# Forming each difference product at its own token in a kernel of two attention layers

## The chip, the core and the metric

The kernel runs on one core of a Trainium2 chip. A core has a matrix engine (PE), a vector engine (DVE), a scalar engine (ACT), a general engine (POOL) and a queue engine (SP) that issues transfers. Each works through its own instructions in order, and they wait for one another by semaphores. The metric is the device time of one execution in microseconds (us).

## The reference

Two attention layers read the same input, 2048 tokens of width 576, in 32 heads of width 18. Layer A is ordinary multi-head attention; layer B has queries per head and one shared key and value. A gate per token mixes the two.

```python
def _A_ref(x, wqkv, wo):
    B, S, D = x.shape
    H = 32; Dh = D // H
    qkv = ...                                   # (3, B, H, S, Dh)
    q, k, v = qkv[0], qkv[1], qkv[2]
    scores = jnp.einsum("bhqd,bhkd->bhqk", q, k) * Dh ** -0.5
    p = _softmax(scores, axis=-1)
    o = jnp.einsum("bhqk,bhkd->bhqd", p, v)
    return o.transpose(0, 2, 1, 3).reshape(B, S, D) @ wo
# _B_ref: the same with k = x @ wk and v = x @ wv shared by all heads
g = _sigmoid((x * gate_w).sum(-1, keepdims=True))
return g * a + (1 - g) * b
```

## The kernel before, in words

A head of either layer is a unit `u`, 64 in all: 0 to 31 of layer B, 32 to 63 of layer A. A unit has 16 steps, so there are 1024 steps.

Softmax needs a maximum per query row, and it is found by its own pass over the scores. For step M (128 queries of a unit) four products of 54 x 128 by 54 x 512 give the scores against all 2048 keys, 512 keys each. The DVE reduces each product to one maximum per query (`tensor_reduce` into `mx`, L634). The DVE has less room than it would need for this, so every even step hands part of it to ACT. The keys of quarter 1 minus those of quarter 0 lie ready (`kd`); the product with them, the **difference product**, is the score difference. ACT takes its relu into `xb` (L628; two buffers), and the DVE then reads the plain product of quarter 0, adds `xb` and takes the maximum in one instruction (L631): max(a, b) = a + relu(b − a). A pair of steps thus needs one difference product (`x`), one product of quarter 0 that is added to it (`y`), and six plain ones (`m`).

The second pass, LEAD = 22 steps behind, forms the scores again, transposed, four products of 56 x 512 per step (`s`, L670; two extra rows subtract the maximum), lets ACT take the exponential into `pt` (L678), and multiplies `pt` with the values into the accumulator bank `acc` (L685). That last product, here called the sums, is cut into quarters of 128 columns.

PE works in two modes. For scores and maxima the array is split in two halves by rows: the `s` products lie in the lower half, `x`, `y` and `m` in the upper one, and two products run side by side. For the sums it is split into four by columns. Products leave PE through seven banks of the accumulator memory; the eighth is `acc`. Projections of layer A and the output projection are woven in as **units of work**: either as half products on both halves of the array (`A` and `B`, L882, two banks held open), or whole (`U`, 12 products that use all 128 rows, L863).

**What sets the order.** The program is written out in order by hand: `emit` (L1061) reads a string of tokens, one letter per product and a digit for that many quarters of sums. One string covers 8 steps of scores and 4 pairs of maxima, and one pass over it is here called an **emission**; a **group** is the stretch of tokens up to and with a digit. The loop of L1120 runs 125 emissions: 2 PLAIN, 32 HALF14, 1 PLAIN, 42 HALF14, 2 PLAIN, 32 HALF12, 7 PLAIN, 7 DENSE. HALF14 and HALF12 carry one unit of work as half products, DENSE four whole ones, PLAIN none. Groups counted below are those of the strings: group 5 of HALF14 is the long one with most `A` and `B`, group 7 is "yssmsm 2"; group 7 of HALF12 is the long one.

**Where x and y stand in the code.** In `emit`, an `x` token forms a difference product only if none is open (L1072, `pos["x"] == pos["y"]`); if one is open the token does nothing. A `y` token first forms a difference if none is open, and then its own product. `step_max` (L613) writes the product and the instruction that empties its bank.

**Which bank a product takes.** `Clock` (L45) keeps an estimate of when each of the seven banks comes free, from fixed times for a product, an exponential and a reduction; `bank` (L87) takes the one that is free first and books the new use on ACT or the DVE. A `y` is booked as a plain `m`, without its difference. The estimate runs only while the program is written. On the chip a product waits for its bank's last reader, and as PE works in order, everything behind it waits too.

Other work that hangs on the emissions: at fixed steps `begin` issues loads of queries, keys and differences (SP), pieces of normalising (DVE, POOL, SP) and the weights of the output projection.

Of the kernel before, what the change touches and what calls it, by code (L numbers as in the profile page):

```python
# [38 lines left out]
class Unit:  # L39
    def __init__(self, ops, n, dst, done, view=lambda f: f, how="copy"):  # L40
        self.ops, self.n, self.dst, self.done, self.view, self.how = ops, n, dst, done, view, how
        self.left, self.fp = {"a": 0, "b": 0}, {}


class Clock:  # L45


    def __init__(self):
        self.free = [0.0] * 7
        self.t = self.act = self.dve = self.last = 0.0  # L50
        self.mode, self.begun, self.tail = "", [0.0, 0.0], [0.0, 0.0]
        self.turns, self.count, self.held = {"s": 0, "m": 0}, 0, {}

    def turn(self, which):
        n = self.turns[which]
# [30 lines left out]

    def bank(self, what, tile):  # L87
        k, free = self.first()
        if what in "smx":
            s = self.matmul(tile, free, STREAM)  # L90
            act = what != "m"
            self.leave(k, s, act, EXP_T if act else RED_T, EXP_D if act else RED_D)
        else:
            if self.mode == "s":
                self.t = max(self.tail)
            s = max(self.t, free) + (LOAD + 14 * (HALF_MM + 11) if what != "t" else STREAM)
            self.t, self.mode = s + 99, ""
            self.leave(k, s - STREAM, what == "U", COPY_T, COPY_T + 90)
        return k
# [33 lines left out]
def gated_mix_kernel(ctx: ExitStack, tc: tile.TileContext, xT, wall, wv, wo, out):  # L133
# [45 lines left out]
    clk = Clock()  # L179

    def bank_tile(k):
        return ps_b.tile([P, 512], F32, name=f"bank{k}")

    def in_turn(which):
        return bank_tile(clk.turn(which))
# [118 lines left out]
    def run(gen):  # L304
        for _ in gen:
            pass
# [295 lines left out]
    def kst(u):  # L602
        return ksb if u < H else L["ks"][(u - H) % 3]
# [7 lines left out]
    MX = {}  # L611

    def step_max(u, i, c, low=False, which=None):  # L613

        if u not in MX:
            MX[u] = mxs[u] if u < 2 else mxs[2 + u % 3]
        b = SB if low else MB
        if c == "x":  # L620
            k = L["kd", u if u >= H else 0][b:b + 54, :]
        else:
            k = kst(u)[b:b + 54, c * 512:(c + 1) * 512]
        pm = in_turn(which) if which else bank_tile(clk.bank("x" if c == "x" else "m", 1))
        nc.tensor.matmul(pm, qs[u % 3][b:b + 54, i * P:(i + 1) * P], k, start=True, stop=True)  # L625
        if c == "x":
            MX["x", u, i] = lead.tile([P, 512], F32, name="xb", bufs=2)
            nc.scalar.activation(MX["x", u, i], pm, AF.Relu)  # L628
        elif c == 0 and ("x", u, i) in MX:
            junk = lead.tile([P, 512], BF16, name="junk", bufs=1)  # L630
            nc.vector.tensor_tensor_reduce(junk, pm, MX.pop(("x", u, i)), 1.0, -3e38, op0=OP.add, op1=OP.max,  # L631
                                           accum_out=MX[u][:, i, c:c + 1])
        else:
            nc.vector.tensor_reduce(MX[u][:, i, c:c + 1], pm, axis=AX.X, op=OP.max)  # L634
# [22 lines left out]
    def bank(n):  # L657


        u, r = divmod(n, 64)  # L660
        if u < NU - 1:
            return u, r // 4, r % 4
        half, r = divmod(r, 32)
        return u, r // 2, 2 * half + r % 2

    def step_scores(u, i, c, alone, k):

        b = MB if alone and k % 2 else SB
        ps = in_turn("s") if alone is None else ring("s", b == SB)
        nc.tensor.matmul(ps, kst(u)[b:b + 56, i * P:(i + 1) * P],  # L670
                         qs[u % 3][b:b + 56, c * 512:(c + 1) * 512], start=True, stop=True)
        PT["q"] = PT.get("q", []) + [(c, ps)]
        if alone and k == 0:
            return
        for c, ps in PT.pop("q"):
            n = PT["n"] = PT.get("n", -1) + 1
            pt = L["pt"][n % 14 > 3].tile([P, 512], F32, name="pt")
            nc.scalar.activation(pt, ps, AF.Exp, scale=SCALE)  # L678
            PT[u, i, c] = pt
# [262 lines left out]
    NSTEP = 16 * NU  # L942
# [6 lines left out]
    def next_unit():  # L949
        while todo:  # L950
            u = next(todo[0], None)
            if u is not None:
                return u
            todo.pop(0)
# [36 lines left out]
    def keep_busy():  # L991

        for n in (512, 256):
            nc.tensor.matmul(acc[:, 0:n], ident_r[SB:SB + 56, :], ident_r[SB:SB + 56, 0:1].to_broadcast([56, n]),
                             start=True, stop=True, skip_group_check=True)

    def first_steps(ops):

        for op in ops.replace(" ", ""):
            if op == "f":  # L1000
                keep_busy()
            elif op == "s":
                step_scores(*bank(pos["s"]), None, 0)
                pos["s"] += 1
            else:
                M, c = banks.pop(0)
                step_max(*divmod(M, 16), c, op == "l", "m")
# [3 lines left out]
    pos = {"s": 0, "P": 0, "x": (LEAD + 2) // 2, "y": (LEAD + 2) // 2}  # L1011
    for v in range(16):
        if v == 11:
            max_rows(0)
        mt, c, w = next(left)
# [24 lines left out]
    PLAIN = "mssmsm 4 smsmsm 3 smmssx 3 smmsys 3 mssxysm 3 msxmssm 3 mssysms 3 msssmys 4 msmsms 3 smxssm 3"  # L1040
    HALF14 = "ysmssm 4 xsmsms 4 sysmms 4 sAmsAsAsm 3 msAsmBBAABsAABABmsABABmsABABmBBAxBBBx 1 smsysm 4 yssmsm 2 msms 2 msmsms 4 sxsmms 4"
    HALF12 = "mssmsx 4 mssmsm 4 smssyms 4 msmssm 4 msmssm 4 sysmms 3 mssAAmBAAsAABsAABmBsAABmBBABAxBBmBBysxs 3 smsysm 3 smsmxs 3"
    DENSE = "Umssysm 4 smsmsm 3 smsx 5 msmsmsUsxmssy 5 smsmsmUmssyms 4 smsmms 4 sxmssm 7 smsmmsUsyxsms"
    plain = [(M, c) for p in range((LEAD + 2) // 2, NSTEP // 2)
             for M, c in [(2 * p, 2), (2 * p, 3)] + [(2 * p + 1, c) for c in range(4)]]

# [14 lines left out]
    def emit(ops, units=0):  # L1061
        for op in ops.replace(" ", ""):
            if op == "s":
                if pos["s"] % 8 == 0:
                    begin(pos["s"] // 4)
                step_scores(*bank(pos["s"]), pos["s"] // 4 >= NSTEP - LEAD, pos["s"] % 4)
                pos["s"] += 1
            elif op == "f":
                keep_busy()
            elif op in "xy":  # L1070

                if pos["x"] == pos["y"] and 2 * pos["x"] < NSTEP:  # L1072
                    step_max(*divmod(2 * pos["x"], 16), "x")
                    pos["x"] += 1
                if op == "y":
                    step_max(*divmod(2 * pos["y"], 16), 0)
                    pos["y"] += 1
            elif op == "m":
                M, c = plain.pop(0)
                step_max(*divmod(M, 16), c)  # L1080
            elif op in "AB":
                if units:
                    half_step(op.lower())
            elif op == "U":
                u = next_unit() if units else None
                if u:
                    whole_unit(u)
                    units -= 1
            elif op == "V":
                whole_unit(next(out_last))  # L1090
            elif op in "abc":
                if op == "a":
                    while slow:
                        run(slow.pop(0))
                    L["half"] = last_sums(pos["P"] // (4 * NSTEP))
                next(L["half"])
                if op == "a" and not pos["P"] // (4 * NSTEP):
                    next(out_last)
            else:
                n = 1 if op == "P" else int(op)  # L1100
                while n:
                    last, h = divmod(pos["P"], 4 * NSTEP - 64)
                    if last:
                        k = min(n, 2 - h % 2)
                        last_pv(h // 32, h % 32 // 2, 128 * (h % 2), 128 * (h % 2 + k))
                    else:
                        T, a = divmod(pos["P"], 4)
                        k = min(n, 4 - a)
                        step_pv(*divmod(T, 16), 128 * a, 128 * (a + k))
                    pos["P"] += k  # L1110
                    n -= k
                    if pos["P"] % 64 == 0 and pos["P"] < 4 * NSTEP:
                        head_out(pos["P"] // 64 - 1)
# [3 lines left out]
    open_ph2()  # L1117
    begin(0)
    first_steps("smf smf smf smf")
    while pos["s"] < 4 * (NSTEP - LEAD):  # L1120
        T = pos["s"] // 4
        if (T + LEAD) % 16 == 0 and (T + LEAD) // 16 - 1 < NU:
            max_rows((T + LEAD) // 16 - 1)
        if T >= SEG[1][3] + 4:
            emit(DENSE, 4)
        elif VB <= T < VB + 8 * 32 or RB <= T < RE:
            emit(HALF14, 1)
        elif SEG[0][3] + 4 <= T < SEG[0][3] + 4 + 8 * 32:
            emit(HALF12, 1)
        else:  # L1130
            emit(PLAIN)
# [45 lines left out]
```

## Time and profile before

| | |
|---|---|
| median of three runs | 2784.67 us (2784.38 to 2785.37) |
| the profiled execution | 2785.18 us, its span 2783.4 us |
| granted clock of TensorE | 1.00 |
| before the loop's first scores | about 135 us |
| the 125 emissions | from about 135 to 2714 us |
| the end (last scores, sums, projection) | 69.5 us |

The page gives busy time per engine as a share of the span. A PE that is busy is not PE at its peak: products of the two halves overlap, and a product that waits for its bank shows as a late load of weights (PEld) behind an idle time. The chain of waits is the work that ended last, followed back; it is read in order of time, each row with its start, its length, the engine, what it writes and its line. In the timeline a row has start, length, engine, line, operation, tiles and shapes, the count merged, and in brackets the idle time of the engine before it and what ended it.

### The profile page before, as it was taken

To read this page: it belongs to the slowest core of one execution; us is meant where nothing else is said; L and a number is where in the kernel's file an instruction comes from. 1 tells how busy PE (TensorE), PEld (TensorE's weight loads), DVE (VectorE), ACT (ScalarE), POOL (GpSimd) and SP (SyncE) were. 2 spreads that over 40 slices of the span, in tenths; PEclk is the share of its full clock that TensorE was granted. 3 is DMA by queue.
4 is the path that set the end of the run, shared out by engine and by line. 5 is a ranking of instruction groups with operands and counts; after the bars stand their busy time and mean duration, and the time that the engine had idled before them with its cause. 6 is when DMAs were issued, how large, how long until landed. Compare 5 with 4: busy or idle time off the path is not lost.

```text
span 2783.4 us, 61929 instructions
## 1 busy us (share of the span) xinstructions
PE 2759.3 (99%) x23256; PEld 1367.6 (49%) x23256; DVE 2427.6 (87%) x4559; ACT 2440.9 (88%) x4787; POOL 425.5 (15%) x633
## 2 busy tenths in 40 slices
PE   9999999999999999999999999999999999999999
PEld 7644444444444444444444444454444544445555
DVE  5889999999999999999999999899888988998773
ACT  4399999999999999999999999999999999997776
POOL 2710000010003112322222122000100010101002
PEclk9999999999999999999999999999999999999999
DMA  8821111321124344434555453222321231233312
GB/s 275 331 64 57 56 48 46 82 70 44 57 67 148 110 125 139 134 121 134 167 159 174 132 147 122 83 72 85 101 80 58 81 99 57 70 95 108 99 37 88
DMA packets 190128, 293.71 MB, mean 106 GB/s; under 512 B 54738, under 2 KB 149282, under 8 KB 178252
## 3 DMA queue, kind: packets, MB, share of 16 engines
q1 hardware_dynamic: 170564, 224.02, 27.5%
q0 software_dynamic: 18368, 64.50, 6.2%
q8 instruction: 183, 3.00, 0.4%
q10 hardware_dynamic: 896, 1.23, 0.1%
q14 instruction: 117, 0.96, 0.1%
HBM read 203.29 MB, written 77.62 MB: 101 GB/s over the span
## 4 chain that ended last, share of the span: by engine, by line
PE 88%; DVE 6%; ACT 3%; issue 2%; DMA 1%; POOL 0%; SPq 0%; ACTq 0%; POOLq 0%; DVEq 0%
PE acc L685 34%; PE bank L670 21%; PE bank L625 21%; PE bank L882 7%; DVE junk L631 3%; ACT xb L628 3%; PE bank L863 2%; PE bank L251 2%; DVE mx L634 2%; ACT pt L678 1%; PE acc L697 0%; DMA qs<-qk 0%; SPq L139 0%; DMA qk<-phl 0%; PE bank L361 0%
## 5 line engine op out<-in xcount | busy, mean ns | idle before, releaser
L678 ACT ACTIVATE pt<-bank 128x512 f32<-128x512 f32 x4096 | 2147.8, 609 | 208.1 <-PE bank L670 112.7
L634 DVE TENSOR_REDUCE mx<-bank 128x1 f32<-128x512 f32 x3096 | 1965.2, 684 | 119.1 <-PE bank L670 61.7
L670 PE MATMUL bank<-qs,ksb 56*128 56x512 f32 x2688 | 913.5, 430 | 8.2
L625 PE MATMUL bank<-ksb,qs 54*128 54x512 f32 x2364 | 799.6, 420 | 2.4 <-DVE mx L631 1.0
L670 PEld LDWEIGHTS bank<-qs,ksb 56*128 56x128 f32 x2688 | 438.7, 184 | 279.6 <-DVE mx L634 158.1
L685 PE MATMUL acc<-pt,vb 128*19 128x512 f32 (+3 forms) x5240 | 565.8, 506 | 0.0
L685 PE MATMUL acc<-pt,vg 128*19 128x256 f32 (+3 forms) x5688 | 537.2, 469 | 0.0
L625 PEld LDWEIGHTS bank<-ksb,qs 54*128 54x128 f32 x2364 | 399.1, 184 | 246.4 <-ACT pt L678 130.3
L670 PE MATMUL bank<-qs,ksa 56*128 56x512 f32 x1408 | 468.3, 434 | 3.7 <-DVE ksb L215 0.5
L631 DVE CUSTOM_DVE_ANT_0 junk<-bank,xb 128x512 bf16<-128x512 f32 x500 | 343.2, 686 | 136.8 <-ACT xb L628 94.3
L625 PE MATMUL bank<-ksa,qs 54*128 54x512 f32 x1232 | 425.8, 425 | 1.8 <-DVE mx L631 1.1
L628 ACT ACTIVATE xb<-bank 128x512 f32<-128x512 f32 x500 | 305.8, 612 | 34.4 <-PE bank L670 33.6
L670 PEld LDWEIGHTS bank<-qs,ksa 56*128 56x128 f32 x1408 | 223.7, 184 | 144.4 <-ACT pt L678 56.4
L625 PEld LDWEIGHTS bank<-ksa,qs 54*128 54x128 f32 x1232 | 207.1, 184 | 151.0 <-ACT pt L678 84.0
L213 POOL CAST mh<-mt 128x32 fp32r<-128x32 f32 x64 | 13.5, 211 | 1470.6 <-DVE mt L643 1470.6
L685 PEld LDWEIGHTS acc<-pt,vg 128*19 128x19 f32 x5688 | 110.6, 97 | 202.3 <-issue 180.0
L685 PEld LDWEIGHTS acc<-pt,vb 128*19 128x19 f32 x5240 | 90.3, 97 | 195.0 <-issue 182.1
L625 PE MATMUL bank<-kdb,qs 54*128 54x512 f32 x372 | 170.3, 458 | 0.0
L882 PE MATMUL bank<-xr,wrh 64*128 64x292 f32 (+1 forms) x756 | 145.7, 300 | 0.0
L625 PEld LDWEIGHTS bank<-kdb,qs 54*128 54x128 f32 x372 | 68.5, 184 | 115.9 <-ACT pt L678 56.0
L882 PEld LDWEIGHTS bank<-xr,wrh 64*128 64x128 f32 x756 | 124.6, 186 | 0.1
L882 PE MATMUL bank<-vwh,xv 64*128 64x288 f32 x576 | 109.4, 298 | 0.0
(142 smaller groups left out, 1917.8 us busy)
## 6 DMA issues: line engine op xcount, KB each, us to landing
qs<-qk SPq DMA_DIRECT2D x384, 144.0 KB
xr<-x_d SPq DMA_DIRECT2D x36, 1314.0 KB
ksa<-qk SPq DMA_DIRECT2D x132, 144.0 KB
qk<-phl POOLq DMA_DIRECT2D x32, 512.0 KB, 5.4
qk<-rhl POOLq DMA_DIRECT2D x36, 292.0 KB, 3.3
ksb<-qk SPq DMA_DIRECT2D x66, 144.0 KB
xv<-x_d SPq DMA_DIRECT2D x16, 576.0 KB
onh<-oh POOLq DMA_DIRECT2D x32, 256.0 KB, 3.7
```

The costliest lines, as they stand in the source:

```text
L213: eng_h.tensor_copy(h, src)
L251: nc.tensor.matmul(fp[:, p0:p0 + g], w[a][:kr, k, :], X[b][:kr, k, x0 + p0:x0 + p0 + g], start=(n == 0), stop=(n == len(PROJ) - 1))
L625: nc.tensor.matmul(pm, qs[u % 3][b:b + 54, i * P:(i + 1) * P], k, start=True, stop=True)
L628: nc.scalar.activation(MX["x", u, i], pm, AF.Relu)
L631: nc.vector.tensor_tensor_reduce(junk, pm, MX.pop(("x", u, i)), 1.0, -3e38, op0=OP.add, op1=OP.max, accum_out=MX[u][:, i, c:c + 1])
L634: nc.vector.tensor_reduce(MX[u][:, i, c:c + 1], pm, axis=AX.X, op=OP.max)
L670: nc.tensor.matmul(ps, kst(u)[b:b + 56, i * P:(i + 1) * P], qs[u % 3][b:b + 56, c * 512:(c + 1) * 512], start=True, stop=True)
L678: nc.scalar.activation(pt, ps, AF.Exp, scale=SCALE)
L685: nc.tensor.matmul(acc[32 * j:32 * j + 19, a:b], v_of(u, i), PT[u, i, j][:, a:b], start=(i == 0), stop=(i == 15), skip_group_check=True)
L863: nc.tensor.matmul(fp[:, 0:u.n], x, y, start=(n == 0), stop=(n == len(u.ops) - 1))
L882: nc.tensor.matmul(u.fp[op][:, 0:u.n], x[b:b + 64], y[b:b + 64], start=(n == 0), stop=(n == len(u.ops) - 1))
```

## The change

An `x` token now forms a difference product whether or not one is open, so up to two are ahead, as many as there are `xb` buffers; one is formed ahead of the loop, and only a `y` token still looks whether one is open. The bank estimate has a kind `y` of its own: it keeps a list of the times at which it reckons the relus to be done, and a `y` starts on the DVE no earlier than its own. The strings PLAIN, HALF14 and HALF12 are as before. DENSE is rewritten as four equal pairs.

```diff
     def bank(self, what, tile):
         k, free = self.first()
-        if what in "smx":
+        if what in "smxy":
             s = self.matmul(tile, free, STREAM)
-            act = what != "m"
+            act = what in "sx"
+            if what == "y" and self.diffs:
+                self.dve = max(self.dve, self.diffs.pop(0))
             self.leave(k, s, act, EXP_T if act else RED_T, EXP_D if act else RED_D)
+            if what == "x":
+                self.diffs.append(self.free[k])
...
-        pm = in_turn(which) if which else bank_tile(clk.bank("x" if c == "x" else "m", 1))
+        pm = in_turn(which) if which else bank_tile(clk.bank("x" if c == "x" else "y" if c == 0 and ("x", u, i) in MX else "m", 1))
...
-    DENSE = "Umssysm 4 smsmsm 3 smsx 5 msmsmsUsxmssy 5 smsmsmUmssyms 4 smsmms 4 sxmssm 7 smsmmsUsyxsms"
+    DENSE = "smsysm 4 smsmsmUsmsx 4 smsysm 4 smsmsmUsmsx 4 smsysm 4 smsmsmUsmsx 4 smsysm 4 smsmsmUsmsx 4"
...
-                if pos["x"] == pos["y"] and 2 * pos["x"] < NSTEP:
+                if (op == "x" or pos["x"] == pos["y"]) and 2 * pos["x"] < NSTEP:
                     step_max(*divmod(2 * pos["x"], 16), "x")
                     pos["x"] += 1
...
     first_steps("smf smf smf smf")
+    emit("x")
     while pos["s"] < 4 * (NSTEP - LEAD):
```

The strings that keep their text:

```python
PLAIN = "mssmsm 4 smsmsm 3 smmssx 3 smmsys 3 mssxysm 3 msxmssm 3 mssysms 3 msssmys 4 msmsms 3 smxssm 3"
HALF14 = "ysmssm 4 xsmsms 4 sysmms 4 sAmsAsAsm 3 msAsmBBAABsAABABmsABABmsABABmBBAxBBBx 1 smsysm 4 yssmsm 2 msms 2 msmsms 4 sxsmms 4"
HALF12 = "mssmsx 4 mssmsm 4 smssyms 4 msmssm 4 msmssm 4 sysmms 3 mssAAmBAAsAABsAABmBsAABmBBABAxBBmBBysxs 3 smsysm 3 smsmxs 3"
```

More of the change, by code (lines that the diff above doesn't have):

```diff
@@ L51, in __init__ @@
         self.mode, self.begun, self.tail = "", [0.0, 0.0], [0.0, 0.0]
-        self.turns, self.count, self.held = {"s": 0, "m": 0}, 0, {}
+        self.turns, self.count, self.held, self.diffs = {"s": 0, "m": 0}, 0, {}, []
     def turn(self, which):
```

## The prediction

> **What bounds the kernel now.** I read the page's totals first, then the waits, then the busy time by stage, and last the chain of work inside one emission of each pattern.
>
> ```profile
> PE 2759.3 (99%) x23256; PEld 1367.6 (49%) x23256; DVE 2427.6 (87%) x4559; ACT 2440.9 (88%) x4787; POOL 425.5 (15%) x633
> ...
> PE 88%; DVE 6%; ACT 3%; issue 2%; DMA 1%; POOL 0%; SPq 0%; ACTq 0%; POOLq 0%; DVEq 0%
> PE acc L685 34%; PE bank L670 21%; PE bank L625 21%; PE bank L882 7%; DVE junk L631 3%; ACT xb L628 3%; PE bank L863 2%; PE bank L251 2%; DVE mx L634 2%; ACT pt L678 1%; PE acc L697 0%; DMA qs<-qk 0%; SPq L139 0%; DMA qk<-phl 0%; PE bank L361 0%
> ```
>
> PE is busy 99% and carries 88% of the chain. But the chain leaves PE for one pair of instructions: the relu of a difference (ACT xb L628, 3%) and the DVE maximum that reads it (junk L631, 3%). 3% of 2783.4 us is 83 us, at 0.69 us each some 120 passages: about one in each of the 125 emissions. The waits say the same:
>
> ```profile
> DVE junk L631 <- ACT xb L628: 94.3, 122, 1.2
> ```
>
> 122 of the 500 `y` products wait for their difference, 0.77 us each. The stages show how much room each engine has:
>
> ```profile
> core 0: us, PE busy (x) PEld busy (x) DVE busy (x) ACT busy (x) POOL busy (x), PEclk, DMA share, GB/s
> 176.40:824.80 648.40, 645.12 (x5506) 305.14 (x5504) 590.84 (x1113) 599.55 (x1185) 26.61 (x55) 1.00 0.19 57
> 844.90:1697.10 852.20, 847.97 (x7226) 400.42 (x7224) 776.14 (x1462) 787.06 (x1556) 201.98 (x303) 1.00 0.47 141
> 1737.20:2392.70 655.50, 653.10 (x5634) 315.85 (x5633) 588.54 (x1112) 601.25 (x1185) 48.46 (x81) 1.00 0.27 79
> 2392.70:2513.00 120.30, 118.38 (x1107) 53.55 (x1104) 108.25 (x204) 110.94 (x217) 15.33 (x20) 1.00 0.28 78
> 2534.70:2713.90 179.20, 178.16 (x1446) 98.86 (x1442) 138.99 (x260) 131.33 (x252) 7.69 (x13) 1.00 0.24 74
> ```
>
> These are 32 and 42 emissions of HALF14, 32 of HALF12, 6 of PLAIN and 7 of DENSE: 20.26, 20.29, 20.48, 20.05 and 25.60 us each. Of 20.29 us ACT is busy 787.06/42 = 18.74 and DVE 776.14/42 = 18.48. Both have about 1.5 us to give in an emission, so PE, with what it waits for, sets the length. The granted clock is 1.00 in every stage.
>
> **Where the wait sits in HALF14.** The chain inside one emission, from the first product of group 7 on:
>
> ```profile
> 1202.24 0.42 PE bank L625
> ...
> 1202.70 0.61 ACT xb L628
> ...
> 1203.33 0.69 DVE junk L631
> ...
> 1204.03 0.61 DVE mx L634
> ...
> 1204.69 0.50 PE bank L670
> 1205.19 0.56 PE acc L685 x8
> 1205.75 0.43 PE bank L625
> ...
> 1206.18 0.23 PE bank L625
> ...
> 1206.64 0.98 PE acc L685 x8
> 1207.62 0.43 PE bank L670
> ```
>
> An undisturbed group of six products (three on each half of the array) takes 1206.64 − 1205.75 = 0.89 us, and four quarters of sums 0.98. A step of one product on each half is 0.23, so four products take 0.66; two quarters take 0.56. Groups 7 and 8 ("yssmsm 2", "msms 2"; before, an `x` is formed just ahead of the `y`) should take 0.89 + 0.56 + 0.66 = 2.11 us to the start of the second sums. They take 1205.19 − 1202.24 = 2.95. The loss is 0.84 us: the seventh product on a half that already had three (0.23), and the DVE that stands until the relu is done, so that the next banks come free late.
>
> **The change, part by part.**
>
> *No work is added.* `x` and `y` stay 500 each, as do all maxima, exponentials, whole units and DMAs; the list of open differences exists only while the program is written. The `x` ahead of the loop replaces a later one. No queue gets a new transfer, and the first `x` of a new unit is in both versions the last `x` token of an emission, so the loads of queries and keys are as early against it as before: no price for SP's or POOL's queue. POOL only splits operands and adds halves; nothing of it moves.
>
> *HALF14 (74 emissions).* The tokens run y x y x x y y x, starting with one difference open. Before, the second of the two neighbouring `x` (end of group 5, "BBAxBBBx") did nothing, and the `y` of group 7 made its own. After, that `x` is formed in group 5 and the `y` of group 7 finds it ready. Gain at most 0.84. Given back: one product more at the end of group 5, beside half products on the other half of the array; I take half a step, 0.10. And ACT gets a second relu just there, 0.49 us later than its exps would start (the pitch below), which group 6 with three exps in 1.87 us does not quite absorb; I take 0.20 for a bank that comes late in group 7. That leaves 0.54. DVE is late next: with five maxima in groups 7 and 8 (5 × 0.63 = 3.1 us for 2.67 us of PE), it falls 0.45 behind, which seven banks should cover and group 10 with two maxima makes good.
>
> ```profile
> 1203.95 5.70 DVE L634 TENSOR_REDUCE mx<-bank 128x1 f32<-128x512 f32 x9
> ...
> 1209.12 2.57 ACT L678 ACTIVATE pt<-bank 128x512 f32<-128x512 f32 x5
> ```
>
> (Pitch of ACT (2.57 − 0.61)/4 = 0.49; of DVE (5.70 − 0.68)/8 = 0.63.) Bounds: 0.23 if only the balance of the halves is won, 0.84 if nothing is given back. 74 × 0.54 = 40 us, bounds 17 and 62.
>
> *HALF12 (32).* The tokens run x y y x y x y x. Now the first `x` is formed in group 1 (two ahead), and the `y` of group 6 ("sysmms 3") needs none.
>
> ```profile
> 2073.85 0.43 PE bank L670
> ...
> 2074.87 0.60 ACT xb L628
> ...
> 2075.50 0.69 DVE junk L631
> ...
> 2076.25 0.73 PE bank L670 x2
> 2076.98 0.41 PE bank L882 x3
> ...
> 2080.52 0.78 PE acc L685 x16
> ```
>
> Without the wait group 6 takes 0.89 and its three quarters 0.78 (the sums of group 7 are three quarters too); group 7 starts at 2073.85 + 1.67 = 2075.52, and its first two scores are done at 2075.52 + 0.66 = 2076.18, where the trace has 2076.98: a loss of 0.80. Against it stands ACT: group 7 has seven exps, two relus and a copy, 10 × 0.49 = 4.9 us, on 4.9 us of PE (2080.52 − 0.80 − 2075.52 = 4.2, and 0.78 of sums), and the relu moved into group 1 comes right behind groups 8 and 9 with seven ACT instructions (3.4 us) in 3.4 us. I take off 0.2: 0.6 each, bounds 0.3 and 0.8. 32 × 0.6 = 19 us, bounds 10 and 26.
>
> *PLAIN (12).* Two `y` of four follow their `x` at once now (groups 5 and 8).
>
> ```profile
> 2461.13 0.49 PE L625 MATMUL bank<-ksb,qs 54*128 54x512 f32 x1
> ...
> 2461.28 0.69 DVE L631 CUSTOM_DVE_ANT_0 junk<-bank,xb 128x512 bf16<-128x512 f32 x1 [0.80 <-ACT xb L628]
> ...
> 2463.06 0.84 PE L685 MATMUL acc<-pt,vg 128*19 128x384 f32 x8
> ...
> 2465.75 0.50 PE L625 MATMUL bank<-ksb,qs 54*128 54x512 f32 x1
> ...
> 2467.50 1.06 PE L685 MATMUL acc<-pt,vg 128*19 128x256 f32 x16
> ```
>
> Seven or eight products stand in 1.93 and 1.75 us, where 0.89 + 0.23 = 1.12 do: 0.81 and 0.63, 1.44 together. ACT caps it: 110.94/6 = 18.49 busy of 20.05 leaves 1.56. With both engines nearly full I take 1.1, bounds 0.5 and 1.5: 13 us (6 to 18).
>
> *DENSE (7).* The new order is "smsysm 4" and "smsmsmUsmsx 4", four times. A whole unit, and five quarters of sums:
>
> ```profile
> 2592.12 1.79 PE bank L863 x12
> ...
> 2594.80 1.20 PE acc L685 x16
> ```
>
> A pair costs 0.89 + 0.98, then 0.89 + 1.79 + 0.66 + 0.98, together 6.19; four are 24.76 against 25.60. Gain 0.84, 7 × 0.84 = 6 us. Eight runs of sums stand where seven stood. A quarter costs (0.98 − 0.56)/2 = 0.21 (five, 1.20, agree), so a run costs 0.98 − 4 × 0.21 = 0.14 and 0.20 for the longer first step after it (0.43 against 0.23): 0.34 × 7 = 2.4 us, and the 6 us already contain it. The Trainium skill, TensorEngine Tiling (Array Packing), section Key Properties, says that changing the tiling mode drains TensorE, which speaks against this order; by that rule and these rows the DENSE term is 6, and without it 8. The trace agrees: the first product after sums takes 0.43, the later ones 0.23. Bounds 0 (the banks held over a unit run short) and 8 (no price for the run).
>
> *The bank estimate* now lets a `y` hold its bank until its difference is there, and puts DVE's later work behind that. No instruction, but every later choice of bank can differ. The trace of before has no row for it. Nearest rows: an undisturbed step waits 0; a bank that came late cost 0.42 of idle before the load:
>
> ```profile
> 1204.69 0.18 PEld L670 LDWEIGHTS bank<-qs,ksb 56*128 56x128 f32 x1 [0.42 <-DVE mx L634]
> ```
>
> So between −0.42 and +0.42 us per emission and wrong (or mended) choice. I take 0: in the undisturbed groups the present estimate already lets no bank come late, and the new one differs only where a difference is pending.
>
> **The sum.** 40 + 19 + 13 + 6 = 78 us off the profiled execution's 2785.2: 2707, and 0.5 less against the median of 2784.67: 2706. With every loss recovered 62 + 26 + 18 + 8 = 114: 2671.
>
> **The rivals.**
>
> *R1: the wait moves to ACT.* The relus now come in bursts (two in group 5 of HALF14, one before group 2 of HALF12), where ACT has least room, and PE waits for an exp's bank instead. For it: 18.74 of 20.29 us busy. Then the lower bounds hold, 17 + 10 + 6 and 2 in DENSE, 35 us: 2750. The Trainium skill, TensorEngine Tiling (Array Packing), section PSUM Bottleneck, says that tiling speeds up TensorE but not the emptying of PSUM, which may become the bottleneck; over a whole emission the row leaves 1.55 us above ACT, more than the 0.84 sought, so the rule can bind here only for a few groups.
>
> *R2: slower, by the choice of banks.* PE issues in order, so one product whose bank is still held stops both halves and the sums behind it. Price 0.42 a time; the gain of 78 us over 106 HALF emissions is 0.74 each, so from two such waits in every emission on the change loses. With two it is 2785 + 106 × 0.84 − 78 = 2796, with three 2840; I name 2815. Against it: nothing of the kind stands in the undisturbed groups now.
>
> *R3: hidden.* If PE's 99% were all work, nothing would move: 2785. Against it: 0.77 us on 122 occasions, and loads that take 49%.
>
> **How the numbers follow.** The forecast, 2671 to 2730, has 0.60; R1, 2730 to 2770, has 0.24; R3 0.04; R2 0.12. A change of 0.2% (5.6 us) is about what this kernel's measurement tells from none. Faster is 0.60 + 0.24 = 0.84, no change 0.04, slower 0.12. The range from 2670 to 2766 leaves out R2, R3 and the edge of R1.
>
> **What would show it.** HALF14 emissions of about 19.7 us, HALF12 of 19.9, PLAIN of 19, DENSE of 24.8. L631's wait for xb falls from 94.3 us to under 20, and the share of xb and junk on the chain to nearly none. Wrong, if loads before L670 and L625 gather new waits on ACT pt (R1) or on one late bank in each emission (R2), if the relu itself waits for its buffer because two differences are open, or if DVE falls behind in group 8.

## The result, and the profile after

The changed kernel takes 2681.4 us (2679.3 to 2682.7) against 2785.0, a ratio of 0.963 with a 95% interval of 0.961 to 0.964: 104 us faster, where 78 were forecast. Its profiled execution took 2681.64 us with a span of 2679.9.

The totals and the chain of the page, after (line numbers of the changed kernel are four higher: the relu is L632, the maximum with it L635, scores L674, sums L689):

```profile
PE 2668.6 (100%) x23032; PEld 1353.3 (51%) x23032; DVE 2422.7 (90%) x4559; ACT 2413.3 (90%) x4787; POOL 425.0 (16%) x633
...
PE 99%; DVE 0%; DMA 0%; issue 0%; SPq 0%; ACT 0%; DVEq 0%
...
L635 DVE CUSTOM_DVE_ANT_0 junk<-bank,xb 128x512 bf16<-128x512 f32 x500 | 342.2, 684 | 31.1 <-PE bank L629 26.0
```

DVE and ACT are nearly as busy in microseconds as they were (2422.7 against 2427.6, 2413.3 against 2440.9). The chain no longer leaves PE: its 6% on DVE and 3% on ACT are gone. The wait of `junk` for `xb`, 94.3 us before, is gone altogether; what idle time is left before L635 ends with its own product. PE's busy share went from 99 to 100% while the time fell by 3.7%; it tells nothing of how far from its limit PE is.

The stages after, in the windows view (32 and 42 emissions of HALF14, 32 of HALF12, 7 of DENSE; then busy time by engine):

```profile
174.80:803.10 628.30, 628.30 (x5508) 303.37 (x5504) 589.05 (x1113) 592.04 (x1185) 26.57 (x55) 1.00 0.20 59
821.70:1646.50 824.80, 824.80 (x7228) 400.12 (x7224) 773.72 (x1463) 777.51 (x1556) 201.73 (x303) 1.00 0.48 145
1683.60:2305.90 622.30, 622.30 (x5636) 310.58 (x5632) 588.45 (x1113) 594.32 (x1185) 48.42 (x81) 1.00 0.29 83
...
2436.50:2610.20 173.70, 173.70 (x1232) 88.67 (x1231) 140.89 (x264) 131.87 (x252) 7.92 (x15) 1.00 0.26 78
```

Per emission and in all:

| stage | before | after | gain each | emissions | gain | forecast |
|---|---|---|---|---|---|---|
| HALF14 | 20.28 | 19.64 | 0.64 | 74 | 47.5 | 40 |
| HALF12 | 20.48 | 19.45 | 1.04 | 32 | 33.2 | 19 |
| PLAIN (mean of all 12) | 20.12 | 18.68 | 1.44 | 12 | 17.3 | 13 |
| DENSE | 25.85 | 24.81 | 1.04 | 7 | 7.3 | 6 |

The DENSE string of before begins with a whole unit, and the window 2534.70:2713.90 that the prediction took for the stage begins behind the first of them. The table counts that unit to DENSE (181.0 us in place of 179.2) and not to PLAIN. The chain of before shows it:

```profile
2532.37 1.78 PE bank L863 x12
```

The first scores of the loop come 1.5 us later in this execution, and the end is as long as it was. 47.5 + 33.2 + 17.3 + 7.3 − 1.5 is the 104 measured. The 1.5 us are not the price of the difference formed ahead: in the profile of the next kernel below, which forms it too, the first scores come at 134.4 us, in after at 136.3, before at 134.8.

The chain in HALF14 after, from group 7 on, beside the one the prediction showed:

```profile
1148.39 0.42 PE bank L629
...
1149.28 0.56 PE acc L689 x8
1149.84 0.42 PE bank L629
...
1150.58 0.56 PE acc L689 x8
1151.14 0.42 PE bank L629
```

Groups 7 and 8 take 1150.58 − 1148.39 = 2.19 us to the second sums. It was 2.95, and 2.11 was worked out as the undisturbed time.

### The profile page after: what moved, and what is told of

It reads as the page before. It is cut to its first block, busy times and chain, and to the rows that moved or that the text cites. A ratio compares the mean times of both kernels' runs of the same rounds, so it can differ in the third digit from the quotient of the medians.

```text
span 2679.9 us, 61494 instructions
## 1 busy us (share of the span) xinstructions
PE 2668.6 (100%) x23032; PEld 1353.3 (51%) x23032; DVE 2422.7 (90%) x4559; ACT 2413.3 (90%) x4787; POOL 425.0 (16%) x633
## 4 chain that ended last, share of the span: by engine, by line
PE 99%; DVE 0%; DMA 0%; issue 0%; SPq 0%; ACT 0%; DVEq 0%
PE acc L689 38%; PE bank L629 26%; PE bank L674 21%; PE bank L886 7%; PE bank L255 4%; PE bank L867 3%; PE acc L701 1%; DMA wst<-wall 0%; DVE mx L638 0%; DVE oacc L862 0%; PE bank L935 0%; PE bank L302 0%; DVE rl L925 0%; SPq L143 0%; DVE sm L753 0%
## 5 line engine op out<-in xcount | busy, mean ns | idle before, releaser
L674 PE MATMUL bank<-qs,ksb 56*128 56x512 f32 x2688 | 898.6, 429 | 1.5 <-issue 1.5
L629 PE MATMUL bank<-ksb,qs 54*128 54x512 f32 x2364 | 801.5, 423 | 0.1
L674 PEld LDWEIGHTS bank<-qs,ksb 56*128 56x128 f32 x2688 | 438.2, 184 | 258.6 <-DVE mx L638 125.6
L689 PE MATMUL acc<-pt,vb 128*19 128x512 f32 (+3 forms) x5240 | 565.8, 506 | 0.0
L689 PE MATMUL acc<-pt,vg 128*19 128x512 f32 (+3 forms) x5464 | 538.4, 481 | 0.0
L629 PEld LDWEIGHTS bank<-ksb,qs 54*128 54x128 f32 x2364 | 389.4, 184 | 276.2 <-ACT pt L682 129.0
L674 PE MATMUL bank<-qs,ksa 56*128 56x512 f32 x1408 | 460.7, 433 | 0.6 <-DVE ksb L219 0.5
L629 PE MATMUL bank<-ksa,qs 54*128 54x512 f32 x1232 | 426.8, 429 | 0.0
L635 DVE CUSTOM_DVE_ANT_0 junk<-bank,xb 128x512 bf16<-128x512 f32 x500 | 342.2, 684 | 31.1 <-PE bank L629 26.0
L632 ACT ACTIVATE xb<-bank 128x512 f32<-128x512 f32 x500 | 301.3, 628 | 12.0 <-PE bank L674 11.8
L674 PEld LDWEIGHTS bank<-qs,ksa 56*128 56x128 f32 x1408 | 222.7, 184 | 151.7 <-ACT pt L682 83.6
L629 PEld LDWEIGHTS bank<-ksa,qs 54*128 54x128 f32 x1232 | 203.7, 184 | 141.9 <-ACT pt L682 82.5
L689 PEld LDWEIGHTS acc<-pt,vg 128*19 128x19 f32 x5464 | 103.3, 97 | 185.2 <-issue 163.2
L689 PEld LDWEIGHTS acc<-pt,vb 128*19 128x19 f32 x5240 | 90.3, 97 | 189.3 <-issue 176.3
L629 PE MATMUL bank<-kdb,qs 54*128 54x512 f32 x372 | 150.9, 434 | 0.0
L217 POOL CAST rhl<-rst 128x292 fp32r<-128x292 f32 (+2 forms) x54 | 22.6, 418 | 474.2 <-DVE rst L862 436.0
```

Source lines behind the costliest of these rows:

```text
L217: eng_h.tensor_copy(h, src)
L674: nc.tensor.matmul(ps, kst(u)[b:b + 56, i * P:(i + 1) * P], qs[u % 3][b:b + 56, c * 512:(c + 1) * 512], start=True, stop=True)
L689: nc.tensor.matmul(acc[32 * j:32 * j + 19, a:b], v_of(u, i), PT[u, i, j][:, a:b], start=(i == 0), stop=(i == 15), skip_group_check=True)
```

## The experiments

Each kernel is named by its edit; the changed kernel is called "after".

**The token rule alone.**

```diff
 # on the kernel before
-                if pos["x"] == pos["y"] and 2 * pos["x"] < NSTEP:
+                if (op == "x" or pos["x"] == pos["y"]) and 2 * pos["x"] < NSTEP:
...
     first_steps("smf smf smf smf")
+    emit("x")
```

> The kernel before with only the token rule changed (an x always forms a difference, one formed ahead of the loop); the bank estimate and DENSE as before. If the gain comes from differences that are ready when their y arrives: 2681 plus the 6 us of DENSE, about 2687 (2683 to 2697). If it comes from the better bank estimate, which is left out here: above 2730, with waits for late banks in the HALF groups.

2678.5 us (2677.4 to 2678.8), ratio 0.962 (0.960 to 0.963). The whole gain is here, and 3 us more than in after. About half of these lie in the DENSE stage, which takes less with its old string than with the new one.

```profile
819.80:1644.70 824.90, 824.90 (x7228) 400.19 (x7224) 774.11 (x1463) 777.54 (x1556) 202.05 (x303) 1.00 0.48 145
1681.80:2304.10 622.30, 622.30 (x5636) 310.76 (x5632) 588.90 (x1114) 594.44 (x1186) 48.50 (x81) 1.00 0.29 83
2436.40:2606.80 170.40, 170.40 (x1446) 95.39 (x1442) 138.91 (x260) 130.97 (x251) 7.70 (x13) 1.00 0.26 79
```

HALF14 and HALF12 take what they take in after (824.9 and 622.3 against 824.8 and 622.3). DENSE takes 172.2 against 173.7: the window above, 170.4, begins behind the first whole unit, which takes 1.8.

**The bank estimate alone.**

```diff
 # on the kernel before
-        if what in "smx":
+        if what in "smxy":
...
+            if what == "y" and self.diffs:
+                self.dve = max(self.dve, self.diffs.pop(0))
```

(with the list of differences and the kind `y`, as in after)

> The kernel before with only the bank estimate changed (a y is booked behind its difference). If the estimate carries the gain: below 2750. If the differences do: within 6 us of 2785, and the wait of the DVE's junk for xb stays at about 94 us.

2753.2 us (2751.8 to 2753.5), ratio 0.989 (0.987 to 0.990): 32 us, where one theory said 6 at most and the other over 35. The waits of this kernel:

```profile
DVE junk L635 <- ACT xb L632: 93.2, 121, 1.4
```

The wait itself stays (93.2 us, 121 times, against 94.3 and 122). So the estimate takes away none of it; it gives the products behind it banks that do not hang on the late DVE. HALF14 falls to 20.05 us, HALF12 to 20.30. The page's chain, and the chain in HALF14 from group 7 on:

```profile
PE 99%; DVE 0%; DMA 0%; issue 0%; ACT 0%; SPq 0%; DVEq 0%
```

```profile
1190.04 0.42 PE bank L629
...
1191.16 0.56 PE acc L689 x8
1191.72 0.43 PE bank L629
...
1192.63 0.56 PE acc L689 x8
```

Group 7 takes 1.12 us to its sums, as it did before; group 8 takes 0.91 where it took 1.27 (2.95 − 1.12 − 0.56). The DVE stands for `xb` as long as ever, and the chain stays on PE all the same. So it was not the DVE's wait in itself that cost time in group 8, but the product that stood before a bank of the late DVE. A chain that no longer leaves PE is then no mark of the whole gain: here it stays on PE with 32 of the 104 us won. Both theories missed this: the estimate matters as long as differences are late. With the token rule it matters no more, as the run with the old DENSE string in after shows.

**The DENSE string alone.**

```diff
 # on the kernel before: DENSE as in after, nothing else
```

> The kernel before with only the new DENSE string. By the sum of the prediction 6 us faster: 2779 (2776 to 2785), each DENSE emission 24.8 us in place of 25.6. If the extra run of sums costs more than its 0.34 us, or banks run short over the unit: 2785 or more.

2777.9 us (2777.0 to 2778.4), ratio 0.997 (0.996 to 0.998): 7 us, all of it in DENSE, which takes 173.7 us where it took 181.0 with its first unit.

```profile
2532.90:2706.60 173.70, 173.70 (x1231) 88.74 (x1231) 140.88 (x264) 131.90 (x252) 7.90 (x15) 1.00 0.26 77
```

This is what the stage takes in after: with this string the token rule makes no difference to it.

**The old DENSE string in after.**

```diff
 # on the changed kernel: DENSE as before, nothing else
```

> The changed kernel with the DENSE string of before; the token rule and the bank estimate stay. If the new string costs one more run of sums (0.34 us in each of 7 emissions, 2.4 us) and wins nothing once the differences are ready: 2678 to 2679, DENSE 24.5 per emission. If the bank estimate is what made 2678 of the kernel without it: 2681 as the changed kernel.

2678.3 us (2677.8 to 2679.5), ratio 0.962 (0.960 to 0.963). The whole unit at the head of DENSE in the chain, and the window behind it:

```profile
2435.17 1.78 PE bank L867 x12
```

```profile
2437.50:2607.90 170.40, 170.40 (x1446) 95.42 (x1442) 138.95 (x260) 131.01 (x251) 7.68 (x13) 1.00 0.26 78
```

Against after only the string differs. With the whole unit that stands ahead of the window the stage takes 172.2 us against 173.7, 1.5 for the worse by the new string. Five emissions, from the first score of the second to that of the seventh, first in this kernel, then in after:

```profile
2461.41:2584.05 122.64, 122.64 (x1043) 69.10 (x1042) 100.08 (x187) 94.04 (x180) 7.64 (x13) 1.00 0.29 87
```

```profile
2460.61:2584.78 124.17, 124.17 (x884) 63.24 (x880) 100.45 (x187) 94.54 (x181) 7.68 (x13) 1.00 0.28 84
```

That is 24.53 and 24.83 us each: the new string costs 0.30 more. The prediction priced its extra run of sums at 0.34. The medians differ by 3 us; what lies outside the stage was not traced to anything. Against the first run only the bank estimate differs: 2678.3 and 2678.5. Once the differences are ready, the estimate is worth nothing that can be measured. This kernel and the token rule alone are the quickest that do the whole computation; their ratios overlap with that of after.

**The wait or the uneven halves.** In HALF14 before, group 7 carries seven products with four on one half, and a `y` that waits. Here the seven stay, and the `y` stands last.

```diff
 # on the kernel before, in HALF14
-smsysm 4 yssmsm 2 msms 2
+smsysm 4 xssmsmy 2 msms 2
```

> The kernel before, in HALF14 alone group 7 is written x s s m s m y in place of y s s m s m: the difference is still formed in group 7, which keeps its seven products with four on one half, but its y stands five products later. The gain of HALF14 in the changed kernel is 0.65 us in each of 74 emissions, 48 us. If nearly all of it is the DVE's wait: about 0.23 of it stays lost for the seventh product and the rest comes, 0.4 x 74 = 30 us, 2755 (2745 to 2765). If it is the uneven load of the halves: 2785. If the later y only moves the wait to group 8: 2775 or more, with DVE idle before junk still at 0.4 us or more there.

2760.6 us (2759.6 to 2761.8), ratio 0.991 (0.990 to 0.993). HALF14 takes 19.95 us, 0.33 less than before and 0.31 more than after, and the DVE's waits for `xb` fall from 94.3 us (122 times) to 53.2 (50 times). The chain, from group 7 on:

```profile
1166.48 0.42 PE bank L625
...
1167.60 0.56 PE acc L685 x8
1168.16 0.43 PE bank L625
...
1169.05 0.56 PE acc L685 x8
```

Group 7 takes 1.12 us (0.89 with three products on each half), group 8 0.89 (1.27 before, 0.74 in after). So of the 0.64 us gained in after about half is the late DVE, which goes already if the `y` stands five products behind its `x`. It is the same loss in group 8 that the bank estimate alone took away by another way. Most of the rest, 0.23, is the seventh product.

**Less work for DVE.**

```diff
 # on the changed kernel
-nc.vector.tensor_reduce(MX[u][:, i, c:c + 1], pm, axis=AX.X, op=OP.max)
+nc.vector.tensor_reduce(MX[u][:, i, c:c + 1], pm if which else pm[:, 0:256], axis=AX.X, op=OP.max)
```

> The changed kernel, in which the plain DVE maxima of the loop read 256 of their 512 columns, so that the maximum is taken over part of the keys (that part of the computation is left out); products, banks, order and ACT are as they were. DVE loses some 0.25 us of 0.63 on 24 maxima of each emission, about 6 us of 18.4. If PE now sets the length by itself: HALF14 stays at 19.5 to 19.6, PLAIN goes from 18.5 to 18.0 to 18.4, the whole 2668 to 2682. If late banks from DVE still cost: HALF14 under 19.3, the whole under 2655.

2676.8 us (2676.5 to 2678.1), ratio 0.961 (0.960 to 0.963).

```profile
820.00:1643.90 823.90, 823.90 (x7228) 395.34 (x7224) 537.17 (x1462) 777.52 (x1556) 201.83 (x304) 1.00 0.48 146
```

DVE's busy time falls from 773.7 to 537.2 us in 42 emissions, and these take 823.9 in place of 824.8. In this stage DVE holds nothing up any more. The expected fall of PLAIN to 18.4 us or less did not come: an emission between two others takes 18.5, as in after.

**Less work for ACT.**

```diff
 # on the changed kernel: relu, and the maximum that reads it, over 256 of 512 columns
-nc.scalar.activation(MX["x", u, i], pm, AF.Relu)
+nc.scalar.activation(MX["x", u, i][:, 0:256], pm[:, 0:256], AF.Relu)
```

> The changed kernel in which relu and the maximum that reads it take 256 of their 512 columns (the maximum then leaves out half of two quarters of the keys); all else is the same. ACT does some 0.2 us less at each of 4 differences of an emission, DVE 0.27 less. Less DVE alone bought 4 us. If ACT now sets the length, as 0.49 us more of it cost 0.52 us: 0.4 to 0.8 us per emission, 2581 to 2631. If ACT and PE end side by side and PE is the one that remains: 2668 to 2681.

2673.2 us (2672.2 to 2673.6), ratio 0.960 (0.958 to 0.961): HALF14 19.62, HALF12 19.35, and PLAIN 18.32 between two others (18.53 in after). ACT lost 23 us of 778 and DVE 41 of 774 in the 42 emissions below, and they lost 0.6.

```profile
818.80:1643.00 824.20, 824.20 (x7226) 392.99 (x7224) 732.52 (x1462) 754.53 (x1555) 201.89 (x303) 1.00 0.48 146
```

Of the two outcomes expected, it is the one in which PE remains. The last two kernels, with part of the work of DVE and of ACT left out, are 5 and 8 us quicker than after; to take away more was not tried.

**More work for ACT, in a burst and away from it.** Every fourth relu is done twice.

```diff
 # on the changed kernel
             nc.scalar.activation(MX["x", u, i], pm, AF.Relu)
+            if (16 * u + i) // 2 % 4 == 3:        # second run: == 0
+                nc.scalar.activation(MX["x", u, i], pm, AF.Relu)
```

> The changed kernel, in which the relu of every fourth difference (the second of the burst in group 5 of HALF14, the last of group 7 of HALF12) is done twice, into the same buffer: 0.49 us more for ACT in each of 125 emissions, 61 us in all. If ACT has room even in its bursts: up to 15 us slower, 2681 to 2696. If a burst costs as the prediction took it (0.20 us for 0.49): 0.2 x 125 = 25, about 2706. If ACT sets the length: 61 slower, 2740.

> The changed kernel with the relu of every fourth difference done twice, as in the run before it, but of the one formed in the last groups of each emission (group 10 of HALF14, group 9 of HALF12, groups 10 of PLAIN), away from the burst of group 5. If the 65 us that the repeat cost there were the price of a burst: under 20 us here, 2681 to 2700. If ACT has no room anywhere in an emission: about 61 us again, 2740 to 2750.

2747.2 us (2746.7 to 2747.8) and 2751.7 us (2750.6 to 2752.7). 61 us more for ACT cost 66 and 70 us, in the burst and away from it alike: 0.5 to 0.6 us in each emission, but 0.3 in those of DENSE. Yet ACT is busy 802.46 us of the 846.3 in this stage of the first of the two, 95%:

```profile
839.50:1685.80 846.30, 846.30 (x7226) 393.96 (x7224) 779.27 (x1462) 802.46 (x1598) 201.52 (x303) 1.00 0.47 142
```

The chain of the first in HALF14 group 7, and two loads of weights from the timeline of that group:

```profile
1174.39 0.43 PE bank L629
...
1175.41 0.49 PE bank L629
1175.89 0.56 PE acc L691 x8
```

```profile
1174.91 0.18 PEld L629 LDWEIGHTS bank<-ksb,qs 54*128 54x128 f32 x1 [0.29 <-ACT pt L684]
...
1175.39 0.18 PEld L629 LDWEIGHTS bank<-ksb,qs 54*128 54x128 f32 x1 [0.30 <-ACT pt L684]
```

The group takes 1.50 us in place of 0.89. The chain stays on PE in it, and two products stand 0.29 and 0.30 us before a bank that ACT's exponentials held. Over the whole execution ACT has 5% of the chain of the first kernel and 2% of that of the second.

**The same, with the bank estimate told.** The difference that is read twice is booked with 477 ns more on ACT.

```diff
 # on the first of the two kernels above; "z" is such a difference
+            more = EXP_T if what == "z" else 0
-            self.leave(k, s, act, EXP_T if act else RED_T, EXP_D if act else RED_D)
+            self.leave(k, s, act, EXP_T + more if act else RED_T, EXP_D + more if act else RED_D)
```

> The repeated relu of the first such run (2747), with the bank estimate told of it: that difference is booked with 477 more for ACT and its bank that much longer. If the 65 us came from a bank that the estimate thought free while ACT still read it: most of it goes, 2685 to 2710, and group 7 of HALF14 is back at 0.9 to 1.1 us from 1.5. If ACT itself or the number of banks is what ran out: 2735 to 2750.

2724.3 us (2723.8 to 2724.9), between the two expectations.

```profile
1182.21 0.43 PE bank L630
...
1183.28 0.56 PE acc L692 x8
1183.83 0.43 PE bank L630
...
1184.70 0.56 PE acc L692 x8
```

Group 7 is back at 1.07 us, as one theory said, but group 8 takes 0.87 in place of 0.74. Of the 66 us, 23 came from banks that the estimate took to be free; 43 remain, 0.34 us of time for 0.49 us of ACT. ACT has no share of this kernel's chain (PE 99%).

**The copy of a half sum on DVE in place of ACT.**

```diff
 # on after with the old DENSE
-                leave_unit(u, u.fp["a"], "copy")
+                nc.vector.tensor_copy(u.dst, u.view(u.fp["a"][:, 0:u.n]))
```

(and the estimate books it on DVE)

> The changed kernel with the DENSE string of before (2678.3), and in HALF14 and HALF12 the first half sum of each unit copied out by DVE in place of ACT, the bank estimate told so. ACT does 0.46 us less just ahead of its two relus in each of 106 emissions, DVE 0.45 more. If ACT's burst still holds PE up: HALF14 and HALF12 fall by 0.05 to 0.2 us each, 2657 to 2673. If PE sets the length by itself now: 2675 to 2681. If DVE, at 18.4 of 19.6 us, has no room for it: 2685 or more.

2701.3 us (2700.2 to 2701.8), 23 us slower than without. HALF14 takes 19.80 us and HALF12 19.76, 0.17 and 0.31 more. The loads of weights for the products of the upper half (L629) wait longer for DVE. Here, then without the edit:

```profile
PEld bank L629 <- DVE mx L638: 209.0, 356, 0.8
```

```profile
PEld bank L629 <- DVE mx L638: 132.4, 213, 0.8
```

So DVE has no room for 0.45 us at that place, though 0.23 us less on each of its maxima had bought nothing. The estimate also gives out the banks in another order here, and what that costs by itself was not tried.

**DENSE with half products.**

```diff
 # on the changed kernel, DENSE; the copied half sum in the buffer of "oe"
-smsysm 4 smsmsmUsmsx 4
+smsysm 4 smsmsmABABABABABABABABABABABABsmsx 4
```

> The changed kernel, in DENSE the four whole units written as twelve half products on each half of the array (A and B in turn) at the same place of the string, so the array does not change to 128 rows and back. A unit took 1.79 us; twelve steps of half products 12 x 0.134 = 1.61. With 0.1 to 0.2 us more for the changes of mode saved, four units give 1.0 to 1.6 us of 24.8 per emission, 7 to 11 us: 2671 to 2675. Against it: ACT copies four half sums more per emission (4 x 0.43) and two banks are held open for 1.6 us; if that binds, 2681 or more.

2689.2 us (2686.4 to 2689.6), 8 us slower than after; DENSE takes 25.8 us. The group with the unit takes 3.43 us up to its sums where the whole unit took 3.34, so the steps of half products cost no less than the whole ones with their changes of mode. They were expected to take 1.61 us; where the chain shows all 24 in one piece, they take 2.07:

```profile
2489.17 2.07 PE bank L886 x24
```

The rest of the loss is at least partly the choice of the buffer: in the waits of this stage ACT stands up to 3.4 us for the transfer out of it (us in total, times, longest).

```profile
ACT tmp L897 <- DMA sum_d<-oe: 5.3, 2, 3.4
```

## Why the prediction was right, and where it was off

*The mechanism.* Right. The token rule alone gives the gain, the wait for `xb` is gone, and PE carries 99% of the chain. Every term but the estimate's came out larger than forecast, 104 us in place of 78. HALF12 passed its upper bound by 7 us, and the total stayed inside the range because the other terms kept below theirs. R2 and R3 are out. R1 (the wait moves to ACT) is out too: no stage shows only its lower bound.

*HALF14, 40 us: measured 47.* The loss of 0.84 us was read rightly; 0.30 was booked as given back and 0.20 was. The longest group went from 3.27 to 3.32 us to its sums, so the product at its end cost 0.05 and not 0.10. For a late bank in group 7 0.20 was booked; none came late there (0.89 us), but group 8 takes 0.74 in place of 0.66. The remaining 0.07 is spread over the other groups. Of the split of the loss, the 0.23 for the seventh product is borne out (1.12 us against 0.89). Of the 0.61 put down to the wait, the run with the late `y` won 0.38 in these two groups and the bank estimate alone 0.36; the other 0.15, in group 8, came only when the seventh product had gone too.

*HALF12, 19 us: measured 33, above its upper bound of 26.* Two terms were mis-sized. The loss was read as 0.80 and was 1.06, and 0.20 was taken off for ACT where 0.05 was given back. The 0.80 counted 0.66 us of work from the first product of group 7 to its first half products, as if these had to stand behind two scores. In after they start 0.34 us behind the group's first product, beside the second score. Before, their load stood for a bank of the late DVE as well. Before, then after:

```profile
2075.69 0.50 PE L625 MATMUL bank<-ksb,qs 54*128 54x512 f32 x1
...
2076.85 0.29 PEld L882 LDWEIGHTS bank<-woh,oih 64*128 64x128 f32 x3 [0.31 <-DVE mx L634]
2076.86 0.53 PE L882 MATMUL bank<-woh,oih 64*128 64x288 f32 x3
```

```profile
2005.46 0.50 PE L629 MATMUL bank<-ksb,qs 54*128 54x512 f32 x1
...
2005.80 0.61 PE L886 MATMUL bank<-woh,oih 64*128 64x288 f32 x3
```

This part of the group takes 1.17 us before and 0.34 after, 0.83 less; group 6, without its seventh product, takes 0.23 less. From the first half product to the sums of group 7 it is 3.6 us in both, so that part was rightly taken as work. What was given back shows in group 9, 0.98 us in place of 0.92; whether ACT is its cause was not tried.

*PLAIN, 13 us: measured 17.* The loss of 1.44 us was found, and cut to 1.1 for engines that are nearly full. All of it came. The same misjudgement as with ACT in HALF12: being busy 92% was read as giving back part of the gain, and next to nothing was given back.

*DENSE, 6 us: measured 7.* The sum of 24.76 us per emission stands against 24.81. What it was compared with was off twice. The 25.60 of before leaves out the first whole unit of the stage, as said above; with it, it is 25.85. And it was a DENSE that waits for a difference too. That wait goes with the token rule, which leaves 24.53 for the old string, so that the new string by itself costs 0.30 per emission. The prediction had the price of the extra run of sums (0.34), but the two edits' gains were added although they heal the same wait.

*The bank estimate, 0.* Right in this combination (2678.3 against 2678.5 us), for the reason given: it differs only where a difference is pending. How much that can be was not seen: alone it would have been worth 32 us.

*What would have shown it wrong.* One of the signs came, and weakly: the loads before the scores wait 175.1 us for ACT's exponentials, before 136.4. With the token rule alone it is 129.1, so this does not come from the early differences; in that kernel DENSE has its old string. The others did not come: what idle time ACT has before L632, 11.8 us in all, ends with its product and not with its buffer. And a DVE that falls behind would have shown in the run that halves its maxima, which won 0.02 us per emission of HALF14.

*Left open.* With more work on ACT, 43 us remain that the estimate does not explain. Whether it is the number of banks or the order of the tokens that keeps ACT's idle 5% from taking up added work was not tried.

## What to carry to other kernels

Where the chain leaves the busiest engine for the same short detour once in every round, sum the detour with the undisturbed groups of the same trace; engines that are 92% busy beside it, and 94% after, need not take much of the gain back. Before adding up stages, look where each window begins: here one whole unit lay on the wrong side. Edits that heal the same wait are not to be added: each alone was worth something here (107, 32 and 7 us), and together 104. And a price is good for one sign only: what costs its full length when it is added may bring nothing when it is taken away.

## What the runs showed of the hardware that was not expected

The three engines end close together. Half a microsecond more on ACT in an emission of 19.6 us costs 0.5 us (0.34 in the mean when the choice of banks is told of it), and 0.45 more on DVE (with 0.46 less on ACT) 0.17 to 0.31. But 5.6 us less on DVE (236.6/42) gains 0.02, and 0.55 less on ACT (23/42) with 0.98 less on DVE (41.2/42) 0.01. So the 6% for which ACT and DVE stand idle did not take up the work that was added. In the one group that was looked at, a product that stands before its bank holds up PE, and with it the products that both are to read; that it is so in every emission is not shown.
